# First unit of a chunked-attention and MLP kernel: the order of the first up matmuls, the engine of two query copies, the place of the roots and the steps of the next tiles' attention

## The chip, the cores and the metric

The kernel runs on one core of a Trainium2 chip. The metric is the device time of one execution in microseconds. A profile also has a span, from the first to the last instruction on the core; the time of an execution of the kernel before is 1.7 to 1.9 us longer than its span. Positions in time below are microseconds from the start of the span.

TensorE multiplies matrices, ScalarE and VectorE work on what it leaves in PSUM and on SBUF, GpSimd issues most loads and computes small things, and SyncE issues the stores. In the profile they are PE (PEld for its weight loads), ACT, DVE, POOL and SP; a "q" after a name is the engine's sequencer.

## The reference

A chunked attention with memory keys feeds a block of normalization, two matmuls and a residual:

```python
# attention, per chunk of 32 queries: 8 memory keys, 16 left, 32 own, 8 right
scores = scale * q_c @ k_full.T            # batch 4, heads 8, seq 768, head_dim 64
a = softmax(scores);  out_c = a @ v_full
# block on x = attention output as (4, 768, 512)
mu, var = mean(x), mean((x - mu) ** 2)
xn = (x - mu) / sqrt(var + 1e-6) * g_ln
out = x + relu(xn @ w_ch1) @ w_ch2         # 512 -> 2048 -> 512, float32 out
```

## The kernel before

The 3072 rows are 24 tiles of 128, worked off as 8 units of 3 tiles. Within a unit, steps 0 to 15 are the *up* steps: step hc makes hidden block hc, 128 of the 2048 hidden features for the unit's 384 rows, from four matmuls. Steps 16 to 27 are the *down* steps. Between them TensorE does the attention of the following unit's tiles: scores, values, a normalization on VectorE (`norm`), a transpose (`turn_x`), as its plan says. In the first unit, hidden blocks 0 to 7 are made before the steps begin, for one row tile at a time, as the tiles' attention ends. The *root* of a tile gives 1/sqrt(var), which is only wanted when the tile's output is added up.

```python
    def root(t, xi):
        i = t % 3
        nc.scalar.activation(out=junk, in_=xs[xi], func=ACTF.Square,
                             bias=nmean[i], accum_out=squares[i])
        nc.gpsimd.tensor_scalar(out=veps[i], in0=squares[i], ...)
        nc.gpsimd.tensor_tensor(out=rstd[xi], in0=veps[i], in1=mhalf, op=ALU.pow)

    def up(u, n, hc, t0=0, on_act=False):      # rows 128*t0 .. 128*n of the unit
        lo, hi = 128 * t0, 128 * n
        p = slot("mm")[:, 0 : hi - lo]         # four PSUM banks in turn
        for dt in range(4):
            nc.tensor.matmul(out=p, lhsT=..w1c[hc // 4].., rhs=xT[u % 2][:, dt, lo:hi], ...)
        # rectification to rT[hc]: ScalarE if hc is odd or on_act, else VectorE
    # ...
    turn_x(0, 0, 0, "mm")
    stay_busy(3)
    values(0, 2)
    norm(2, 2)
    for hc in range(3):
        up(0, 1, hc, 0, True)
    turn_x(0, 1, 1)
    for hc in range(3, 8):                     # block 4 needs w1c[1]
        up(0, 1, hc, 0, True)
    for hc in range(2):
        up(0, 2, hc, 1, True)
    turn_x(0, 2, 2)
    for hc in range(2, 8):
        up(0, 2, hc, 1)
    for hc in range(8):
        up(0, 3, hc, 2)
    # ... plan of the first unit
            at(7, clear_q, 1, 0)
            at(9, clear_q, 1, 1)
            at(10, clear_k, 1)
            for j in (0, 2):
                at(15, kq_block, 0, j, 6, NG, "mm")   # transposes of keys and queries,
                at(15, keep_rest)                     # copies out: keys VectorE, queries ScalarE
            for t in range(3):
                at(8 + t, root, t, t)
            # ... loads of the next batch
            attend(((17, 20, 20, 22), (18, 22, 22, 24), (21, 24, 24, 27)), "att")
    # attend: for each following tile the steps of scores, values, norm, turn_x;
    # its root three steps after turn_x, at the latest in step 27
```

Scores, values and transposes share two PSUM tiles, `att`, in turn: whoever comes next waits until the one before the last has been read. The up weights come in four quarters, `w1c[0]` to `w1c[3]`, each for four blocks.

The softmax here doesn't subtract the row's maximum and nothing guards it: scores larger than these inputs give would overflow.

Of the kernel before, what the change touches and what calls it, by code (L numbers as in the profile page):

```python
# [15 lines left out]
def kernel(  # L16
# [12 lines left out]
    nc = tc.nc  # L29
# [3 lines left out]
    NG = 12  # L33
# [47 lines left out]
    att = [ps.tile([128, 2, 512], FP32, name=f"att{i}") for i in range(2)]  # L81
    mm = [ps.tile([128, 512], FP32, name=f"mm{i}") for i in range(4)]
    turn = {"att": 0, "mm": 0}

    def slot(kind):
        lst = {"att": att, "mm": mm}[kind]
        turn[kind] = (turn[kind] + 1) % len(lst)
        return lst[turn[kind]]
# [4 lines left out]
    def free(ap, off, pattern, parts=None):  # L93

        p = list(ap.ap[0]) if parts is None else [ap.ap[0][0], parts]
        return bass.AP(tensor=ap.tensor, offset=ap.offset + off, ap=[p] + [list(x) for x in pattern])

    def as16(t):
        return t.bitcast(FP16)
# [75 lines left out]
    def turn_kq(pv, src, j, n):  # L175

        for r in range(8):
            for par in range(2):
                nc.tensor.matmul(  # L179
                    out=pv[64 * par : 64 * par + 64, n * r : n * r + n],  # L180
                    lhsT=src[0:n, 2 * j + par, r, :],
                    rhs=identity[0:n, 0:n],
                    is_transpose=True, start=True, stop=True,
                    tile_position=(0, 64 * par),
                )
# [14 lines left out]
    def keep_q(copy, pv, b, j, par, n, g0, g1):  # L200


        rows = slice(64 * par, 64 * par + 64)
        copy(  # L204
            out=free(QZ[b % 2][rows, g0, j, par, :], 0, [[512, g1 - g0], [8, 8], [1, 8]]),
            in_=free(pv[rows, :], 8 * g0, [[8, g1 - g0], [1, 8], [n, 8]]),
        )

    def kq_block(b, j, g0, g1, kind):

        pk, pq = slot("att"), None
        if kind == "att":
            pq = slot("att")
            pq = [pq[:, i, :] for i in range(2)]
        else:
            pq = [slot("mm")[:, :] for i in range(2)]
        for i in range(2):
            turn_kq(as16(pk[:, i, :]), k16[b % 2], j + i, 96)
        for i in range(2):
            turn_kq(as16(pq[i]), q16[b % 2], j + i, 96)  # L220

        def keep(i):
            keep_k(as16(pk[:, i, :]), b, j + i, 96, g0 + 1 if g0 else 0, g1)
            for par in range(2):
                keep_q(nc.scalar.copy, as16(pq[i]), b, j + i, par, 96, g0, g1)

        keep(0)
        kept_later.append(lambda: keep(1))
# [133 lines left out]
    def stay_busy(n, p=None):  # L362

        p = slot("mm") if p is None else p
        for _ in range(n):
            nc.tensor.matmul(out=p, lhsT=busy[:, 0:128], rhs=busy, start=True, stop=True)
# [3 lines left out]
    def up(u, n, hc, t0=0, on_act=False):  # L370

        lo, hi = 128 * t0, 128 * n
        p = slot("mm")[:, 0 : hi - lo]
        c, i = hc // 4, hc % 4
        for dt in range(4):
            w = w1c[c][:, dt, :]
            nc.tensor.matmul(  # L377
                out=p, lhsT=free(w, i, [[4, 128]]), rhs=xT[u % 2][:, dt, lo:hi],
                start=(dt == 0), stop=(dt == 3),
            )  # L380
        o = rT[hc][:, lo:hi]
        if hc % 2 or on_act:
            nc.scalar.activation(out=o, in_=p, func=ACTF.Relu)  # L383
        else:
            nc.vector.tensor_scalar(out=o, in0=p, scalar1=0.0, scalar2=None, op0=ALU.max)  # L385
# [170 lines left out]
    for hc in range(3):  # L556
        up(0, 1, hc, 0, True)
    turn_x(0, 1, 1)
    for hc in range(3, 8):
        up(0, 1, hc, 0, True)  # L560
    for hc in range(2):
        up(0, 2, hc, 1, True)
    turn_x(0, 2, 2)
    for hc in range(2, 8):
        up(0, 2, hc, 1)
    for hc in range(8):
        up(0, 3, hc, 2)

# [2 lines left out]
    for u, tiles in enumerate(units):  # L571
        n = len(tiles)
        following = units[u + 1] if u + 1 < len(units) else []
        plan = {}

        def at(step, fn, *args):
            plan.setdefault(step, []).append((fn, args))

        def attend(steps, kind="dma"):

            for i, (s0, s1, s2, s3) in enumerate(steps):
                t = following[i]
                at(s0, scores, t // 6, t % 6)
                at(s1, values, t // 6, t % 6)
                at(s2, norm, t % 6, t % 9)
                at(s3, turn_x, u + 1, i, t % 6, kind)
                at(min(s3 + 3, 27), root, t % 6, t % 9)

        def cross(steps, b, t0, t1, t2):

            for half in range(2):
                at(steps[half], cross_k, b, half, t0, t1)
                at(steps[2 + half], cross_q, half, t2 - 3, t2)

        def spread(step, b, t0, t1):
            for half in range(2):
                at(step + half, spread_q, b, half, t0, t1)

        if u == 0:
            at(7, clear_q, 1, 0)  # L600
            at(9, clear_q, 1, 1)
            at(10, clear_k, 1)
            at(23, clear_v, 1, nc.gpsimd)
            for j in (0, 2):
                at(15, kq_block, 0, j, 6, NG, "mm")
                at(15, keep_rest)
            for t in range(3):
                at(8 + t, root, t, t)
            for h in (0, 4):
                for which in range(2):  # L610
                    at(15, load_kq, 1, which, 0, 96, h, h + 4)
            for g in range(6):
                at(23, load_v_group, 1, g)
            attend(((17, 20, 20, 22), (18, 22, 22, 24), (21, 24, 24, 27)), "att")
            at(26, mem_cols, 1)
            at(26, v_mem, 1)
        elif u == 1:
            for j in (0, 2):
                at(5 + 3 * j, kq_block, 1, j, 0, NG, "att")
                at(7 + 3 * j, keep_rest)  # L620
            for g in range(6, NG):
                at(0, load_v_group, 1, g)
            for t in range(6):
                for which in range(2):
                    at(14, load_tokens, 2, which, t)
            attend(((16, 19, 19, 22), (17, 19, 20, 23), (21, 23, 23, 26)), "att")
        elif following:
            if u in (2, 4):
                attend(((2, 7, 7, 7), (4, 7, 8, 8), (9, 13, 13, 13)))
            else:  # L630
                attend(((9, 14, 14, 14), (11, 14, 15, 15), (16, 20, 20, 20)))
            if u == 2:
                cross((0, 0, 1, 1), 2, 0, 4, 3)
                at(8, mem_cols, 2)
                at(8, k_around, 2, 0, 4)
                for h in range(H):
                    at(8, load_v_head, 2, h)
                spread(9, 2, 0, 3)
                cross((14, 14, 15, 15), 2, 4, 6, 6)
            elif u == 3:  # L640
                at(1, v_mem, 2)
                at(1, v_around, 2)
                at(4, k_around, 2, 4, 6)
                spread(5, 2, 3, 6)
                for t in range(6):
                    for which in range(2):
                        at(24, load_tokens, 3, which, t)
            elif u == 4:
                for h in range(H):
                    at(0, load_v_head, 3, h)  # L650
                cross((14, 14, 15, 15), 3, 0, 4, 3)
                at(17, mem_cols, 3)
                at(17, v_mem, 3)
                at(17, v_around, 3)
                at(22, k_around, 3, 0, 4)
                spread(23, 3, 0, 3)
                cross((20, 21, 24, 25), 3, 4, 6, 6)
            elif u == 5:
                at(2, k_around, 3, 4, 6)
                spread(3, 3, 3, 6)  # L660
        for step in range(16 + 4 * n):
            if step < 16:
                if u or step > 7:
                    up(u, n, step)
            else:
                i, part = divmod(step - 16, 4)
                if u == 0:
                    i, part = (step - 16) % 3, (step - 16) // 3
                if following or i < n - 1:
                    down(tiles[i], i, part)  # L670
                elif part == 0:
                    down_last(tiles[i], i)
            for fn, args in plan.get(step, ()):
                fn(*args)
# [30 lines left out]
```

## Time and profile before

| | before |
|---|---|
| time, median (range) of 4 runs | 219.86 us (219.46 to 220.27) |
| span of the profile | 218.0 us |
| TensorE busy | 209.7 us, 96% |
| first up matmul | 17.92 |
| key transposes of step 15 begin | 31.13 |
| second unit's up begins | 49.87 |
| last VectorE work ends | 215.24 |

TensorE's busy share says little here: it is the gaps that can be won. The prediction shows its waits, which all lie in the first unit, and what is around them. A wait is best measured by the distance between two starts, less the distance that is normal for the first of them.

### The profile page before, as it was taken

Reading aid. Unit: us, or ns where it says so; the run is one execution under the profiler, and the core shown is the slowest. Engines: PE = TensorE matmul, PEld = TensorE weight load, DVE = VectorE, ACT = ScalarE, POOL = GpSimd, SP = SyncE. Lnnn points to the kernel's source line nnn. Section 1 sums busy time; section 2 is a strip of 40 time slices with the busy share of each in tenths; the row PEclk is TensorE's granted clock in tenths of the full one; section 3 lists DMA queues with packets and bytes.
Section 4 is the critical chain, followed back from the end, with each engine's and each line's share of the span. In section 5 each row is a group of like instructions: output and inputs, shape, how many; then the busy total and the mean of one; then the engine's idle time right before and its main releaser. Section 6 shows DMA issues by size and latency. Waiting matters only on the chain.

```text
span 218.0 us, 5088 instructions
## 1 busy us (share of the span) xinstructions
PE 209.7 (96%) x2025; PEld 129.8 (60%) x2025; DVE 116.7 (54%) x273; ACT 101.0 (46%) x211; POOL 104.7 (48%) x185
## 2 busy tenths in 40 slices
PE   7997989998999999999999999999999999999994
PEld 2556866546775577545764577447754676456553
DVE  6976673375764746723466339415385437534222
ACT  4476758535884766601555077202751165403200
POOL 7992236988794215987002999507047000300000
PEclk9999999999999999999999999999999999999999
DMA  4999999999999156995603999997673200330012
GB/s 78 181 151 206 209 205 184 200 204 226 167 139 173 64 76 144 148 148 191 81 5 96 113 183 157 155 158 102 159 154 96 96 3 13 83 114 11 0 48 99
DMA packets 87714, 27.37 MB, mean 126 GB/s; under 512 B 78297, under 2 KB 84185, under 8 KB 87642
## 3 DMA queue, kind: packets, MB, share of 16 engines
q0 software_dynamic: 62128, 14.38, 76.6%
q1 hardware_dynamic: 25562, 12.66, 26.5%
q8 instruction: 16, 0.26, 0.5%
q14 instruction: 8, 0.07, 0.1%
HBM read 28.84 MB, written 6.29 MB: 161 GB/s over the span
## 4 chain that ended last, share of the span: by engine, by line
PE 83%; POOL 4%; DMA 4%; DVE 4%; ACT 2%; issue 2%; POOLq 0%; DVEq 0%
PE mm L377 37%; PE mm L394 34%; PE att L289 4%; DMA w1c<-in_moe_w_ch_dram 4%; PE att L309 3%; PE att L179 2%; POOL V L117 2%; PE mm L412 2%; DVE QZ L436 1%; ACT QZ L204 1%; PE att L352 1%; DVE xn L329 1%; DVE xs L320 1%; DVE rT L385 1%; POOL qraw L107 1%
## 5 line engine op out<-in xcount | busy, mean ns | idle before, releaser
L377 PE MATMUL mm<-xT,w1c 128*128 128x384 f16 (+1 forms) x576 | 89.1, 309 | 2.4 <-DMA w1c<-in_moe_w_ch_dram 1.2
L394 PE MATMUL mm<-w2c,rT 128*128 128x512 f16 x368 | 83.9, 379 | 0.0
L377 PEld LDWEIGHTS <-w1c 128*128 128x128 f16 x576 | 58.8, 114 | 25.1 <-issue 1.5
L383 ACT ACTIVATE rT<-mm 128x384 f16<-128x384 f32 (+1 forms) x77 | 33.6, 443 | 71.4 <-PE mm L377 49.9
L394 PEld LDWEIGHTS <-rT 128*128 128x128 f16 x368 | 34.8, 98 | 38.3
L385 DVE TENSOR_SCALAR rT<-mm 128x384 f16<-128x384 f32 (+1 forms) x67 | 35.0, 526 | 34.8 <-PE mm L377 34.5
L401 DVE SCALAR_TENSOR_TENSOR osb<-mm,rstd,xs 128x512 f32<-128x512 f32 x23 | 17.1, 749 | 42.0 <-PE mm L394 27.7
L296 ACT ACTIVATE AT<-att,band 104x512 f16<-104x512 f32 x48 | 30.2, 684 | 11.3 <-PE att L289 11.0
L338 POOL TENSOR_SCALAR veps<-squares 128x1 f32<-128x1 f32 x24 | 5.0, 207 | 46.1 <-ACT junk L335 44.6
L117 POOL DMA_DIRECT2D V<-in_v_dram x24 | 18.4, 773 | 10.9 <-DMA w1c<-in_moe_w_ch_dram 7.7
L335 ACT ACTIVATE junk<-xs,nmean 128x512 f16<-128x512 f32 x24 | 17.3, 720 | 7.1 <-DVE nmean L326 6.7
L329 DVE SCALAR_TENSOR_TENSOR xn<-xs,nmean,g_row 128x512 f16<-128x512 f32 x24 | 18.4, 766 | 0.9
L320 DVE SCALAR_TENSOR_TENSOR xs<-att,rec 128x512 f32<-128x512 f32 x24 | 16.6, 691 | 1.0 <-DVE rec L319 0.2
L289 PEld LDWEIGHTS <-KT 128*128 128x128 f16 x192 | 12.7, 98 | 5.1 <-issue 1.4
L277 POOL COPY QZ<-kraw 64x768 f16<-64x768 f16 x16 | 13.5, 846 | 3.6 <-DMA kraw<-qraw 2.9
L289 PE MATMUL att<-QZ,KT 128*128 128x128 f16 x192 | 14.8, 219 | 0.3 <-ACT QZ L204 0.3
L342 POOL TENSOR_TENSOR rstd<-veps,mhalf 128x1 f32<-128x1 f32 x24 | 13.2, 551 | 2.0
L269 POOL COPY KT<-KT 128x128 f16<-128x128 f16 (+4 forms) x16 | 4.6, 320 | 18.3 <-DMA KT<-kraw 13.7
L123 POOL DMA_DIRECT2D V<-in_v_dram x16 | 12.0, 801 | 0.2 <-issue 0.2
L242 POOL DMA_DIRECT2D qraw<-in_q_dram x12 | 11.2, 935 | 1.3 <-PE mm L377 1.3
L242 POOL DMA_DIRECT2D kraw<-in_k_dram x12 | 11.2, 933 | 0.0
L309 PEld LDWEIGHTS <-AT 104*64 104x64 f16 x384 | 7.6, 111 | 6.1 <-ACT AT L296 2.0
(76 smaller groups left out, 134.2 us busy)
## 6 DMA issues: line engine op xcount, KB each, us to landing
out_dram<-osb SPq DMA_DIRECT2D x23, 256.0 KB, 2.4
V<-in_v_dram POOLq DMA_DIRECT2D x36, 96.0 KB, 6.5
w1c<-in_moe_w_ch_dram POOLq DMA_DIRECT2D x4, 512.0 KB, 9.6
w2c<-in_moe_w_ch_dram POOLq DMA_DIRECT2D x4, 512.0 KB, 13.7
kraw<-in_k_dram POOLq DMA_DIRECT2D x12, 128.0 KB, 4.7
qraw<-in_q_dram POOLq DMA_DIRECT2D x12, 128.0 KB, 4.7
qraw<-in_q_dram POOLq DMA_DIRECT2D x3, 384.0 KB, 10.7
kraw<-in_k_dram POOLq DMA_DIRECT2D x3, 256.0 KB, 5.7
```

The costliest lines, as they stand in the source:

```text
L117: nc.gpsimd.dma_start(out=V[b % 2][r : r + hi - lo, g, :, 0:64], in_=dram(v, b * H * HS + lo * D, [[64, hi - lo], [HS, H], [1, 64]]),)
L242: nc.gpsimd.dma_start(out=free(dst, 512 * t, [[64, H], [1, 64]]), in_=dram(src, b * H * HS + 128 * t * D, [[D, 128], [HS, H], [1, 64]]),)
L289: nc.tensor.matmul(out=p[:, gg, 128 * j : 128 * j + 128], lhsT=KT[b % 2][:, (4 * g + j) * KW : (4 * g + j) * KW + 128], rhs=QZ[b % 2][:, g ...
L296: nc.scalar.activation(out=free(a, 32 * c, [[512, 2], [64, 8], [1, 32]], KR), in_=free(p, 32 * c, [[512, 2], [64, 8], [1, 32]], KR), func= ...
L320: nc.vector.scalar_tensor_tensor(out=x.rearrange("p (h d) -> p h d", h=H), in0=free(p, 0, [[128, H], [1, 64]]), scalar=1.0, in1=free(r, 0, ...
L329: nc.vector.scalar_tensor_tensor(out=xn[i], in0=x, scalar=nmean[i], in1=g_row, op0=ALU.add, op1=ALU.mult,)
L335: nc.scalar.activation(out=junk, in_=xs[xi], func=ACTF.Square, bias=nmean[i], accum_out=squares[i],)
L377: nc.tensor.matmul(out=p, lhsT=free(w, i, [[4, 128]]), rhs=xT[u % 2][:, dt, lo:hi], start=(dt == 0), stop=(dt == 3),)
L383: nc.scalar.activation(out=o, in_=p, func=ACTF.Relu)
L385: nc.vector.tensor_scalar(out=o, in0=p, scalar1=0.0, scalar2=None, op0=ALU.max)
L394: nc.tensor.matmul(out=p, lhsT=rT[hc][:, 128 * i : 128 * i + 128], rhs=w2c[hc // 4][:, hc % 4, :], start=(hc == 0), stop=(hc == 15),)
L401: nc.vector.scalar_tensor_tensor(out=o, in0=p, scalar=rstd[t % 9], in1=xs[t % 9], op0=ALU.mult, op1=ALU.add,)
```

## The change

The intent is to take waits off TensorE in the first unit: run only the blocks of the first weight quarter on single row tiles, so that the second quarter has more time to land; spread the query copies over two engines; start the next tiles' attention a step or two earlier; and move the squares of the roots to where ScalarE is thought freer.

```diff
-    def kq_block(b, j, g0, g1, kind):
+    def kq_block(b, j, g0, g1, kind, last=nc.scalar.copy):
 ...
-                keep_q(nc.scalar.copy, as16(pq[i]), b, j + i, par, 96, g0, g1)
+                keep_q(last if i else nc.scalar.copy, as16(pq[i]), b, j + i, par, 96, g0, g1)
 ...
     turn_x(0, 1, 1)
-    for hc in range(3, 8):
-        up(0, 1, hc, 0, True)
-    for hc in range(2):
+    up(0, 1, 3, 0, True)
+    stay_busy(2)
+    for hc in range(4):
         up(0, 2, hc, 1, True)
     turn_x(0, 2, 2)
-    for hc in range(2, 8):
-        up(0, 2, hc, 1)
+    for hc in range(4, 8):
+        up(0, 2, hc)
     for hc in range(8):
         up(0, 3, hc, 2)
 ...
-                at(15, kq_block, 0, j, 6, NG, "mm")
+                at(15, kq_block, 0, j, 6, NG, "mm", nc.vector.tensor_copy if j else nc.scalar.copy)
 ...
-                at(8 + t, root, t, t)
+                at(19 + t, root, t, t)
 ...
-            attend(((17, 20, 20, 22), (18, 22, 22, 24), (21, 24, 24, 27)), "att")
+            attend(((17, 19, 19, 22), (18, 21, 21, 24), (20, 23, 23, 26)), "att")
```

## The prediction

> **What bounds the kernel now.** I first read the page's busy row per slice and its chain of work that ended last.
>
> ```profile
> PE   7997989998999999999999999999999999999994
> ...
> PE 83%; POOL 4%; DMA 4%; DVE 4%; ACT 2%; issue 2%; POOLq 0%; DVEq 0%
> ```
>
> TensorE is nearly always busy and makes up 83% of the chain, so only its idle time can be won without taking work off it. The change touches the first unit alone, which ends at 49.87 us of the 218.0 us span, when the second unit's first up matmul starts. I therefore asked who TensorE waited for between 17 and 82 us (engine, line, releaser: us in all, times, longest).
>
> ```profile
> PE mm L377 <- DMA w1c<-in_moe_w_ch_dram: 1.2, 1, 1.2
> PE mm L377 <- ACT xT L357: 0.7, 1, 0.7
> PE mm L377 <- DVE rT L385: 0.5, 1, 0.5
> PE att L289 <- ACT QZ L204: 0.3, 1, 0.3
> PE att L309 <- ACT AT L296: 0.3, 1, 0.3
> PE att L352 <- DVE xn L329: 0.2, 1, 0.2
> ```
>
> These six waits, 3.2 us in all, are the whole prize. The same view from 49 us to the end shows none but the 0.7 us one at 49.87 us. The modelled end of a matmul lies after the start of the next, so each costs more than it shows; I use distances between starts below. TensorE's timeline places them; I show four, the other two begin at 42.98 and 45.51 us (start, us, line, tile, count, idle before).
>
> ```profile
> 18.84 0.39 PE L377 MATMUL mm<-xT,w1c 128*128 128x128 f16 x4
> 20.39 1.53 PE L377 MATMUL mm<-xT,w1c 128*128 128x128 f16 x24 [1.17 <-DMA w1c<-in_moe_w_ch_dram]
> ...
> 29.74 1.46 PE L377 MATMUL mm<-xT,w1c 128*128 128x384 f16 x8 [0.55 <-DVE rT L385]
> ...
> 36.37 0.44 PE L289 MATMUL att<-QZ,KT 128*128 128x128 f16 x5 [0.32 <-ACT QZ L204]
> ...
> 49.87 4.06 PE L377 MATMUL mm<-xT,w1c 128*128 128x384 f16 x24 [0.67 <-ACT xT L357]
> ```
>
> The first wait is a transfer: the second quarter of the up weights lands at 20.35 us. The third to sixth come from how ScalarE and VectorE work off the attention of the next three tiles. Their own timelines hold what the change moves:
>
> ```profile
> 25.48 0.71 ACT L335 ACTIVATE junk<-xs,nmean 128x512 f16<-128x512 f32 x1
> ...
> 32.41 3.90 ACT L204 COPY QZ<-mm 64x384 f16<-64x384 f16 x8 [0.68 <-PE mm L179]
> ```
>
> ```profile
> 27.94 1.34 DVE L436 MEMSET QZ<- 64x1536 uint32 x1 [0.26 <-issue]
> ...
> 32.12 2.61 DVE L194 COPY KT<-att 128x352 f16<-128x352 f16 x8 [0.97 <-PE att L179]
> ```
>
> ScalarE needs 3.90 us for eight query copies, VectorE is done with its key copies at 34.73 and then idle until 40.33: the second engine has room.
>
> **What the Trainium skill says.** "TensorE: Matmul & The Clock Gate", section "Wait — 56ns, not 53.3ns?", gives warm back-to-back starts as N / 2.4 GHz plus about 2.5 ns: the trace has 55.8 ns for 128 columns and 162.5 ns for 384, which agrees, so 256 columns should take 109 ns (estimate). "ScalarE: Activation LUTs", section "What ACT_TABLE_LOAD costs", gives an activation with a pointer bias as 280 ns + 0.833 ns an element, 707 ns for 512; the squares of the roots took 720 ns, and another 190 ns instruction reads each sum. "DMA: Bandwidth & Descriptors", section "Issuing engines are not separate DMA queues", says that all transfers share 16 engines; the trace has them over 90% busy from about 5 to 48 us, so issuing one earlier need not land it earlier.
>
> **The change part by part.** I follow TensorE through the unit.
>
> *Up, chunk 0 and 1.* Before, hidden blocks 0 to 7 ran for row tile 0, so block 4 needed the second weight quarter: the gap from 19.06 (four matmuls of 56 ns after 18.84) to 20.39 us is 1.33 us. After, blocks 0 to 3 run for tile 0, then two filler matmuls (2 x 0.216 = 0.43, to 19.5), then blocks 0 to 3 for tile 1. That needs the transposed tile 1, whose copy on ScalarE ends at 19.62, so it starts at 19.67. Sixteen matmuls (0.89) and four transposes (0.22) bring 20.78, when the second quarter is there. Blocks 4 to 7 with 256 columns: 16 x 109 ns = 1.74, to 22.52. Eight blocks of tile 2: 32 x 55.8 ns = 1.79, to about 24.33. Before, this point is 25.11. Gain **0.78 us**. The sixteen fewer matmuls matter little, because columns, not count, cost time. The third and fourth quarters (landed 22.89 and 26.10) are needed at 24.33 and 26.93.
>
> *Up, blocks 8 to 15.* VectorE's chain is last rectification, clear (1.34), block 8, clear (1.34), block 10, which frees the bank for block 14. All of it follows from the point just moved, and neither clear is moved. ScalarE loses three squares here, but TensorE did not wait for it. So that wait (0.55 us in the view, 0.71 by starts: 28.87 to 29.74 where 0.16 is normal) **stays** and gain remains 0.78: key transposes at 30.35 instead of 31.13 (their data landed at 27.19 and 28.98), down steps at 33.2 instead of 33.98.
>
> *Query copies.* Two of eight go to VectorE, after its key copies, which then end at 33.95. It took 0.43 us for 256 query elements and 0.52 for 352 key elements, so two of 384 end near 35.0 (estimate). ScalarE, starting at 31.63, ends its six (0.487 apart) at 34.55 instead of 36.31. TensorE comes to the last head pair of the first scores at 35.1: no wait. Starts before are 35.83 and 36.37, 0.54 apart where 0.056 is normal: gain **0.48**. Scores end at 35.38 instead of 36.64.
>
> *Down steps 18 to 27.* Before, 36.64 to 49.87 is 13.23 us. Work in it: ten down steps of four matmuls (0.865 each) 8.65, two score groups 0.90, three value groups 1.17, three transposes 0.69: 11.41. The rest, 1.82, is the three waits (starts out of step by about 0.43, 0.41, 0.83) and small change. After, scores, values and norms come one step earlier, so that only one pair stays tight: values of tile 4 start at 40.15, VectorE needs 0.56 to begin and 1.91 for its norm (39.77 to 40.33 to 42.24 before), done at 42.62, and TensorE arrives at 42.49: 0.18 lost. The last transpose starts at 45.88 and its copy is ready 1.06 later (48.81 to 49.87 before), 46.94, when TensorE finishes the last down step at 46.97. The next unit starts at about 47.0 instead of 49.87. Gain here 1.82 - 0.18 = **1.64**.
>
> *Roots.* Three squares of 0.9 us move into ScalarE's steps 19 to 21, beside six exponentials of 0.63: 35.6 + 6 x 0.63 + 3 x 0.9 = 42.1, copy of tile 3 to 42.65. The values of tile 5 reuse its PSUM bank and come at 42.9. It fits with 0.2 to spare. GpSimd then issues the next batch's query and key loads first and finishes the roots at about 43 rather than 37.9, needed at 45.
>
> Sum: 0.78 + 0.48 + 1.64 = 2.9 us. The remaining units keep TensorE fed, so they only shift. I take off 0.2 for a wait I have overlooked: 219.97 - 2.7 = **217.3 us**, -1.2%.
>
> **The rivals.**
> 1. *ScalarE becomes the bound of steps 19 to 23.* For: 6.5 us of its work in a 7 us stretch, 0.2 us margin, and norm of tile 3 may not overwrite its mean before the first root has read it (38.97 against 39.15). Against: every use has its turn. Delays of 0.5 to 1 us would leave 217.8 to 218.3 us.
> 2. *The weights take over as the wait.* The third and fourth quarters of the down weights landed at 38.88 and 42.24; I need them at 40.54 and 44.15, 1.7 and 1.9 us later. If the loads moved 2.5 us later, 0.6 to 0.8 of the gain would go: 218 us. Against: they are issued before the moved GpSimd work.
> 3. *GpSimd's later work delays the second unit or beyond.* Its clears wait for the third root, so value loads begin at 45.8 rather than 43.4 us and the later loads about 2 us later. They are used from 65 us on and landed by 58 before. I expect nothing; if it bit, the time would stay near 219.5.
> 4. *The clear's wait goes too*, or fewer matmuls save more than I think: 216.5 us.
>
> **Range and chances.** Each part rests on starts in the trace; the unsure terms are rivals 1 and 4, each some 0.8 us, and the runs scatter by 0.4. So 216.5 to 218.4 us. For 2% faster, 215.57 us, a gain of 4.4 us is needed, more than all six waits cost together (4.2 by starts: 1.33 + 0.71 + 0.48 + 0.43 + 0.41 + 0.83), of which the 0.71 stays. Losing 2% would need a new stall of 7 us. Faster 0.03, within 2% 0.96, slower 0.01.
>
> **What would show it.** TensorE's waits after: none for the up weights; a short one for the transposed tile 1 near 19.7; the rectification wait still 0.5; none or under 0.1 for query copies; none over 0.2 for exponentials; the second unit's up at 47.0. Wrong would be a wait on down weights near 40 or 44, on the copy of tile 3, or an idle TensorE after 50 us.

## The result, and the profile after

The changed kernel took 217.93 us, median of 4 runs (217.74 to 218.26), beside 219.86 us. Ratios here are the mean time of one kernel's runs over that of the other's of the same rounds, so not quite the ratio of the medians; it is 0.9914, with a 95% interval of 0.989 to 0.9937. The gain is 1.9 us where the prediction said 2.7 (it started from 219.97, the median of the runs known by then). It lies within the range given, and within 2%.

The page of the changed kernel, busy tenths of TensorE in 40 slices and the chain that ended last:

```profile
PE   7999989999999999999999999999999999999993
...
PE 94%; DVE 3%; ACT 1%; issue 1%; ACTq 0%
```

No transfer is on the chain any more, and TensorE's share of it grew from 83% to 94%. Who TensorE waited for between 17 and 82 us, the view that had six lines before, now has one:

```profile
PE mm L377 <- DVE rT L385: 0.6, 1, 0.6
```

TensorE's timeline answers line by line to the one shown in the prediction (start, us, line, tile, count, idle before):

```profile
19.19 0.39 PE L377 MATMUL mm<-xT,w1c 128*128 128x128 f16 x4
19.42 0.59 PE L366 MATMUL mm<-busy 128*128 128x512 f16 x2
20.03 1.05 PE L377 MATMUL mm<-xT,w1c 128*128 128x128 f16 x16
...
29.31 1.46 PE L377 MATMUL mm<-xT,w1c 128*128 128x384 f16 x8 [0.55 <-DVE rT L385]
...
35.28 0.61 PE L289 MATMUL att<-QZ,KT 128*128 128x128 f16 x8
...
44.33 0.39 PE L352 MATMUL att<-identity,xn 128*128 128x128 f16 x4
...
47.37 4.06 PE L377 MATMUL mm<-xT,w1c 128*128 128x384 f16 x24
```

The wait for the second weight quarter is gone, the one for block 10's rectification stays, the first scores run all eight matmuls without a break, and the second unit begins 2.50 us earlier. ScalarE and VectorE have shared the query copies: ScalarE's eight in 3.90 us became six, VectorE adds its two after the key copies.

```profile
31.98 2.92 ACT L204 COPY QZ<-mm 64x384 f16<-64x384 f16 x6 [0.68 <-PE mm L179]
...
38.45 0.72 ACT L335 ACTIVATE junk<-xs,nmean 128x512 f16<-128x512 f32 x1
```

```profile
27.51 1.34 DVE L436 MEMSET QZ<- 64x1536 uint32 x1 [0.26 <-issue]
...
34.21 1.11 DVE L204 COPY QZ<-mm 64x384 f16<-64x384 f16 x2
```

Laid out by landmarks, with the two later profiles of the same changed kernel (the experiments after_again and after_third):

| | before | after | after_again | after_third |
|---|---|---|---|---|
| TensorE's clock at full speed from | 4.59 | 6.67 | 4.14 | 4.35 |
| first up matmul | 17.92 | 18.27 | 17.92 | 17.92 |
| from there to key transposes | 13.21 | 12.43 | 12.43 | 12.43 |
| from there to second unit's up | 18.74 | 16.67 | 16.66 | 16.66 |
| from there to end of last VectorE work | 165.37 | 165.42 | 165.38 | 165.37 |
| from there to end of span | 2.81 | 3.24 | 3.68 | 3.35 |
| span | 218.05 | 216.03 | 216.06 | 215.73 |

So the first unit became 2.85 us shorter once its first up matmul ran (0.78 + 2.07), the same in all three profiles, which is the sum of the prediction before it took 0.2 off. Units two to eight kept their length within 0.05 us. What is missing lies at the two ends of the program: a later start in one of three profiles, and 0.4 to 0.9 us more after the last arithmetic in all three.

### The profile page after: what moved, and what is told of

Same layout as the page of the kernel before. It is cut to its first block, busy times and chain, and to the rows that moved or that the text cites. A ratio compares the mean times of both kernels' runs of the same rounds, so it can differ in the third digit from the quotient of the medians.

```text
span 216.0 us, 5059 instructions
## 1 busy us (share of the span) xinstructions
PE 210.2 (97%) x2011; PEld 129.8 (60%) x2011; DVE 118.6 (55%) x274; ACT 99.7 (46%) x206; POOL 104.4 (48%) x185
## 4 chain that ended last, share of the span: by engine, by line
PE 94%; DVE 3%; ACT 1%; issue 1%; ACTq 0%
PE mm L377 37%; PE mm L394 37%; PE att L289 5%; PE att L309 3%; PE mm L366 3%; PE att L179 2%; PE mm L412 2%; PE mm L179 1%; DVE QZ L436 1%; ACT AT L296 1%; PE att L352 1%; PE att L366 1%; DVE rT L385 1%; PE mm L539 0%; DVE xn L329 0%
## 5 line engine op out<-in xcount | busy, mean ns | idle before, releaser
L377 PE MATMUL mm<-xT,w1c 128*128 128x384 f16 (+2 forms) x560 | 89.0, 313 | 0.6 <-DVE rT L385 0.6
L383 ACT ACTIVATE rT<-mm 128x384 f16<-128x384 f32 (+2 forms) x74 | 33.1, 453 | 72.4 <-PE mm L377 50.2
L385 DVE TENSOR_SCALAR rT<-mm 128x384 f16<-128x384 f32 (+2 forms) x66 | 34.9, 533 | 33.6 <-PE mm L377 33.5
L342 POOL TENSOR_TENSOR rstd<-veps,mhalf 128x1 f32<-128x1 f32 x24 | 13.7, 571 | 2.0
```

The source lines that it names most:

```text
L377: nc.tensor.matmul(out=p, lhsT=free(w, i, [[4, 128]]), rhs=xT[u % 2][:, dt, lo:hi], start=(dt == 0), stop=(dt == 3),)
L383: nc.scalar.activation(out=o, in_=p, func=ACTF.Relu)
L385: nc.vector.tensor_scalar(out=o, in0=p, scalar1=0.0, scalar2=None, op0=ALU.max)
```

## The experiments

Twelve runs, ten edited kernels and the changed one twice, all with right results, each timed in rounds beside the kernel before. They came in four calls, each on one chip; times that are compared come from one call unless it is said otherwise. All are within 2% of the kernel before. Means that differ by some 0.5 us have intervals that overlap, so the parts are read from distances within the profiles, of which the three profiles of the changed kernel agree within 0.01 us in the first unit. Means of the kernel before were 219.98, 220.04, 219.94 and 219.92 us.

### The changed kernel again: after_again and after_third

No edit.

> The changed kernel once more, to see whether the 0.6 us between forecast (217.3) and result (217.93) is real. Theory A (late start shows now): in the kernel before, the wait for the second weight quarter at 20.3 us absorbs any late start of TensorE; in the changed one nothing does, so the gain is 2.85 us less whatever the first up matmul is later than 17.9 us in that run (0.35 in the profile after, where the clock opened at 6.67 us instead of 4.59). Then the second unit's up starts 29.1 us after the first up matmul again, and the mean gain is 1.9 to 2.6 us. Theory B (the end): the last stores land 0.4 us later in the changed kernel, every time: last VectorE work to the end of the span is again 3.2 us against 2.8 before. Theory C (scatter): the gain comes out at 2.7 or more.

Measured: 217.70 us median of 4, ratio 0.9897 (0.9878 to 0.9915), a gain of 2.3 us.

> The changed kernel a third time, beside the two versions below on one chip. From the two profiles so far: up starts at 17.9 to 18.3 us, the second unit's up 29.1 us later, last VectorE work to the end of the span 3.2 to 3.7 us (2.8 if the last instruction packet comes after the end, as it did in two of six profiles with 4021 rows); mean 217.6 to 218.0 us.

Measured: 217.56 us median of 5, ratio 0.9897 (0.9882 to 0.9913). The first result, 1.9 us, was at the small end; the gain is about 2.2 us. Theory C, scatter alone, wanted 2.7 or more and falls. Theory B's longer end came back both times, 3.7 and 3.4 us. Theory A's late start did not come in these two profiles.

### Undoing one part: up_old, query_old, attend_old, roots_old

**up_old** puts the up order of the first unit back.

```diff
-    up(0, 1, 3, 0, True)
-    stay_busy(2)
-    for hc in range(4):
+    for hc in range(3, 8):
+        up(0, 1, hc, 0, True)
+    for hc in range(2):
         up(0, 2, hc, 1, True)
     turn_x(0, 2, 2)
-    for hc in range(4, 8):
-        up(0, 2, hc)
+    for hc in range(2, 8):
+        up(0, 2, hc, 1)
```

> Only the up part is undone. My working gives that part 0.78 us where TensorE starts early, 0.43 where it starts as in the profile after; the wait for the second weight quarter (about 1.3 us by starts) comes back, and the second unit's up starts near 47.8 whatever the clock did. So 0.4 to 0.8 us slower than the changed kernel. If the weights were no bound (rival: fewer, wider matmuls made the gain), there would be no wait at 20.4 us and the time would still be slower.

Measured: 218.06 us, mean 0.4 us above after_again's. The transfer's wait is back in the list of TensorE's waits:

```profile
PE mm L377 <- DMA w1c<-in_moe_w_ch_dram: 1.6, 2, 1.3
```

In this run the weights landed late (the first up matmul itself waited for its quarter and came at 18.54), and from there to the key transposes it took 13.30 us instead of 12.43. So the wait was the cost, not the count of matmuls. attend_alone, below, shows this once more: it has the old order and its sixteen more matmuls, but in its profile no wait for these weights, and the same distance was 12.08 us.

**query_old** gives the query copies back to ScalarE.

```diff
-                at(15, kq_block, 0, j, 6, NG, "mm", nc.vector.tensor_copy if j else nc.scalar.copy)
+                at(15, kq_block, 0, j, 6, NG, "mm")
```

> Only the query copies go back to ScalarE. My working: the wait of the first scores for QZ comes back at 0.5 us by starts and all that follows moves by it: 0.5 us slower than the changed kernel. Rival: with scores, values and roots packed closer, ScalarE becomes the bound and the loss is over 1 us; or the values wait for exponentials anyway and the loss is under 0.2.

Measured: 218.20 us median, mean 0.5 us above after_again's. Its first up matmul came at 17.92 as there, and its second unit's up at 47.50 instead of 47.01: 0.49 us, the term of the prediction, with the old wait in its old size:

```profile
35.59 0.44 PE L289 MATMUL att<-QZ,KT 128*128 128x128 f16 x5 [0.33 <-ACT QZ L204]
```

**attend_old** puts the steps of the attention back, and leaves the roots in the down steps.

```diff
-            attend(((17, 19, 19, 22), (18, 21, 21, 24), (20, 23, 23, 26)), "att")
+            attend(((17, 20, 20, 22), (18, 22, 22, 24), (21, 24, 24, 27)), "att")
```

> Only the steps of scores, values, norms and transposes go back, the roots stay in the down steps. My working: a wait of about 0.35 us before the transpose of tile 4 and one of about 0.85 us for the copy of tile 5 before the second unit's up, which starts about 1.0 us later than in the changed kernel: 1.0 us slower. Rival: the earlier query copies and the earlier up already removed these waits, then under 0.3 us.

Measured: 219.78 us, ratio 1.0002: nearly everything is lost, 2.3 us of mean. From the key transposes to the second unit's up it took 18.33 us instead of 16.66, so 1.67 us where I expected 1.0. The two waits that I named are there, and a third. Below are TensorE's lines in the kernel before, then in this run:

```profile
42.98 0.44 PE L309 MATMUL att<-V,AT 104*64 104x65 f16 x16 [0.27 <-ACT AT L296]
...
45.51 0.40 PE L352 MATMUL att<-identity,xn 128*128 128x128 f16 x4 [0.25 <-DVE xn L329]
```

```profile
42.05 0.44 PE L309 MATMUL att<-V,AT 104*64 104x65 f16 x16 [0.29 <-ACT AT L296]
...
44.57 0.40 PE L352 MATMUL att<-identity,xn 128*128 128x128 f16 x4 [0.25 <-DVE xn L329]
...
48.93 1.30 PE L377 MATMUL mm<-xT,w1c 128*128 128x384 f16 x7 [0.67 <-ACT xT L357]
```

With the old steps, the values of tile 4 come second after the scores of tile 5 on the two `att` tiles, so they wait for tile 5's exponentials; with the new steps they take the other `att` tile. The third wait is thus one of the six of the kernel before, with its 0.43 us by starts in the prediction, and my expectation had left it out: 0.43 + 0.41 + 0.83 is 1.67. The squares of the roots, which now stand before these exponentials, are not its cause. ScalarE's lines for the exponentials, before and then here:

```profile
41.67 1.26 ACT L296 ACTIVATE AT<-att,band 104x512 f16<-104x512 f32 x2 [2.25 <-PE att L289]
```

```profile
40.75 1.24 ACT L296 ACTIVATE AT<-att,band 104x512 f16<-104x512 f32 x2
```

They began 0.65 us after the scores of tile 5 (41.02) in the kernel before, where no square stood ahead, and 0.74 us after them (40.01) here, so the squares cost 0.09 us at most. Of the 1.97 us between the spans of the two profiles, 1.67 is this, 0.25 a later start and 0.06 a longer end.

**roots_old** puts the roots of the first three tiles back and leaves all else.

```diff
-                at(19 + t, root, t, t)
+                at(8 + t, root, t, t)
```

> The changed kernel with the roots of the first three tiles back in steps 8 to 10. My working: TensorE waits for none of them at either place, the second unit's up starts 29.1 us after the first up matmul within 0.1, the time is that of the changed kernel within 0.2 us. Rival: their squares delay ScalarE's evictions in the up steps and TensorE loses over 0.3 us there.

Measured: 217.46 us, ratio 0.9883 (0.9862 to 0.9904) beside 0.9897 for the changed kernel: the same. First up matmul to second unit's up is 29.09 us, as in the changed kernel. So moving the roots gave nothing by itself. Nothing in the other parts needed it either.

### One part alone: attend_alone

The kernel before with the new steps of the attention, nothing else.

```diff
-            attend(((17, 20, 20, 22), (18, 22, 22, 24), (21, 24, 24, 27)), "att")
+            attend(((17, 19, 19, 22), (18, 21, 21, 24), (20, 23, 23, 26)), "att")
```

> The kernel before with nothing but the new steps of scores, values, norms and transposes. My working: the waits before the transpose of tile 4 and for the copy of tile 5 and the one for the exponentials go, the others stay; the second unit's up starts near 48.0 instead of 49.87: 1.8 us faster than the kernel before, so most of the gain is this part. Rival: without the earlier query copies ScalarE is late and the new steps wait for it: under 1 us.

Measured: 218.27 us, ratio 0.992, mean 1.7 us below the kernel before. From key transposes to second unit's up it took 17.14 us instead of 18.74: 1.60. Together with the 0.49 us of query_old that is 2.09, beside 2.07 to 2.08 us of the whole change after the key transposes. The parts add up.

This run also shows what theory A says, by accident. Its clock opened at 5.21 us and fell back to half between 12.04 and 15.45, so its up began 1.2 us late:

```profile
19.12 0.86 PE L377 MATMUL mm<-xT,w1c 128*128 128x128 f16 x12
...
20.04 1.94 PE L377 MATMUL mm<-xT,w1c 128*128 128x128 f16 x28
...
31.20 0.87 PE L179 MATMUL att<-identity,kraw 96*64 96x96 f16 x32
```

It has the old up order, and its key transposes came at 31.20, only 0.07 us later than in the kernel before: there was no wait for the second weight quarter this time, the 28 matmuls of the second line, block 4's among them, run through. In the old order the wait takes up a late start. In the new order the distance to the key transposes is 12.43 us whenever the start is, so a late start costs its full length. This is shown for the old order by one profile, and for the new order by the profiles with starts at 17.92 and 18.27.

attend_alone's fall of 3.4 us made its mean clock 0.992; without such a fall no profile lies under 0.996. In the old order the executions at 0.989 to 0.992 are no slower than the others of their kernel: five of the kernel before, mean 219.92 us beside 219.98, one of up_old, 217.92 beside 218.16, and attend_alone's own, 218.39 beside 218.33. In the new order each is the slowest of its kernel or, in pad_free below, one of the two slowest: query_old 219.28 us beside 218.00, attend_old 221.29 beside 219.70, pad_rows 218.32 beside 217.52, pad_free 218.28 and 218.50 beside 217.28. So it cost 0.8 to 1.6 us there and nothing in the old order, as theory A has it; where in the execution the clock fell is on record for attend_alone alone. One of clear_nofill at 0.994 fits: 218.30 us beside 216.88.

### The wait that stayed: clear_later

The second clear of the query buffer goes from the up steps to a down step.

```diff
-            at(9, clear_q, 1, 1)
+            at(18, clear_q, 1, 1)
```

> The second clear of the query buffer moves from step 9 to step 18, where VectorE is idle for some 3 us. My working: the wait for block 8's to 10's rectification (0.71 us by starts) is gone, the second unit's up starts 0.7 us earlier after the first up matmul (28.4 us instead of 29.1), 0.6 to 0.8 us faster than the changed kernel. Rival: the clear delays the norm of tile 3 and the gain is given back: under 0.3 us.

Measured: 217.19 us, ratio 0.9866 (0.9844 to 0.9889). From the first up matmul to the second unit's up it took 28.39 us instead of 29.09: 0.70. The mean is 0.4 us below roots_old's, less than I expected, and the intervals overlap. The wait for block 10's rectification, the only one left in the changed kernel, was the two clears of 1.34 us on VectorE, as the prediction said of it.

### The end of the program: pad_rows, pad_free

SyncE's timeline has the last three stores as one entry: the start of the first issue and the time until the last issue is done. In the kernel before, then in after_again:

```profile
213.67 1.93 SPq L421 DMA_DIRECT2D out_dram<-osb  x3
```

```profile
210.82 2.81 SPq L421 DMA_DIRECT2D out_dram<-osb  x3
```

Issuing a store takes 0.33 us. In after_again one of the three took 1.56 (minimum, median and maximum in ns, then the first and last start):

```profile
L421 SPq DMA_DIRECT2D out_dram<-osb x3: 332/382/1558, 210.8 to 213.2; - x3
```

The last store, whose data was ready at 212.39, was issued at 213.24. The trace's packet records show what flew meanwhile: one instruction packet of 16,384 bytes, from 211.23 to 212.78. There are 16 such packets in an execution, on average some 245 TensorE instructions apart. The Trainium skill, "Runtime: NRT & Kernel Launch", section "Instruction fetch mechanics", says that an engine's instructions are refilled in blocks of 16 KiB, 256 instructions, so these are very likely TensorE's; it says of the cost of crossing such a boundary that it is "mostly hidden". The change made TensorE's program 28 instructions shorter (4021 rows, not 4049, as I counted them; matmuls and weight loads on the pages add up to one more each), which moves the last packet's place against the end: it began 2.04 us before TensorE's last matmul ended in the kernel before, and 0.70, 0.77 and 0.42 us before it in the three profiles of the changed kernel.

**pad_rows** brings the count back to 4049:

```diff
     up(0, 1, 3, 0, True)
-    stay_busy(2)
+    filler = slot("mm")[0:64, 0:64]
+    for _ in range(16):
+        nc.tensor.matmul(
+            out=filler, lhsT=busy[:, 0:64], rhs=busy[:, 0:64], start=True, stop=True
+        )
```

> The changed kernel, with its two fillers of 512 columns turned into sixteen of 64, so that TensorE's program has as many instructions as before the change (4049 rows, not 4021) and nothing else moves. Theory (instruction fetch): in the profiles of the changed kernel the last 16 KB instruction packet flies 0.4 to 1.2 us before TensorE's last matmul, the store issued in it takes 1.1 to 1.6 us to issue instead of 0.33, and the last store waits behind it; in the kernel before, the packet flew 2 us before the end and delayed nothing. With the rows back, the packet goes back to about 2 us before the end, last VectorE work to end of span is 2.8 to 2.9 us instead of 3.2 to 3.7, and the mean is 0.4 to 0.8 us below the changed kernel's 217.7. Rival (scatter): the end varies by itself, the mean is 217.7 within 0.2.

**pad_free** does it where TensorE waits anyway:

```diff
+                if u == 0 and step == 14:
+                    filler = slot("att")[0:64, 0, 0:64]
+                    for _ in range(14):
+                        nc.tensor.matmul(
+                            out=filler, lhsT=busy[:, 0:64], rhs=busy[:, 0:64], start=True, stop=True
+                        )
                 if u or step > 7:
                     up(u, n, step)
```

> The changed kernel with fourteen matmuls of 64 columns put before block 14 of the first unit, where TensorE waits 0.7 us for VectorE anyway: 4049 rows as in the kernel before, and no time of their own. Instruction-fetch theory: the second unit's up still 29.1 us after the first up matmul, the last instruction packet begins 1.9 to 2.0 us before TensorE's end, last VectorE work to end of span 2.8 to 2.9 us, ratio to the kernel before 0.986 to 0.9885 against 0.9897 for the changed kernel. Scatter theory: 0.9885 to 0.991.

Measured in the profiles: the packet began 1.90 and 1.91 us before TensorE's end, no issue was stretched, and the end took 2.79 and 2.81 us. In pad_free:

```profile
210.90 1.93 SPq L421 DMA_DIRECT2D out_dram<-osb  x3
```

Measured in the times: pad_rows 217.60 us (ratio 0.9891), pad_free 217.42 us (0.9902, 0.9877 to 0.9927). The profiled execution of pad_free, 216.99 us, was the fastest of its six; the others went up to 218.50. So the profiles did what the theory said, and the means did not: they are those of the changed kernel, 0.9897. Over all 14 profiles:

| kernels | packet before TensorE's end | last VectorE work to end of span |
|---|---|---|
| 4049 rows: before, up_old, attend_alone, pad_rows, pad_free | 1.90 to 2.04 us | 2.79 to 2.91 us |
| 4041 rows: clear_pad | 1.54 | 3.22 |
| 4021 rows: after, after_again, after_third, attend_old, clear_later | 0.42 to 0.77 | 3.24 to 3.74 |
| 4021 rows: query_old, roots_old; 4017: clear_nofill | after the end | 2.79 to 2.85 |

In the eight profiles with a stretched issue among the last three, it ended 0.36 to 0.37 us after the packet's end, whatever its own length (0.59 to 1.61 us). In three others, pad_rows, pad_free and attend_alone, an issue ran while the packet flew and was not stretched. That a stretched issue ends with the packet is shown by this repeated timing; what holds it back, why some issues escape, and why the packet of three kernels came only after the end, the runs don't show.

Two things lie outside the spans and explain part of the means. First, two of pad_free's six executions, 218.28 and 218.50 us, and one of pad_rows' five, 218.32, had the clock of 0.992 told of above, while none of the changed kernel's 13 was under 0.996. The other four of pad_free have a mean of 217.28 us, 0.988 of the kernel before, which is what the theory said; the other four of pad_rows have 217.52. This choice was made after the fact, so it supports the theory and doesn't show it. Second, a packet after the end is perhaps not free. In seven executions the time is 2.1 to 2.8 us longer than the span. All seven are among the 42 of kernels with 4021 or 4017 rows; there is none among the 72 of the others whose spans are on record. Two of them were profiled, roots_old and clear_nofill, and there the packet ended 2.6 and 2.4 us after the span; in query_old's profile, where it ended 1.6 us after the span, the time is 1.7 us longer as usual. So the short ends of 2.79 us flatter roots_old and clear_nofill, and a span alone can mislead; that the packet is what the execution waited for is not shown.

### The best of both: clear_pad, clear_nofill

clear_pad is clear_later with twelve of the 64-column fillers of pad_rows in place of `stay_busy(2)`; clear_nofill is clear_later without a filler.

```diff
     up(0, 1, 3, 0, True)
-    stay_busy(2)
```

> The later clear (0.71 us) with twelve fillers of 64 columns in place of two of 512, for 4041 rows. If both readings hold, the second unit's up starts 28.4 us after the first up matmul, the last instruction packet flies about 1.5 us or more before TensorE's end, last VectorE work to end of span 2.8 to 2.9 us; mean 216.5 to 217.0 us, 0.8 to 1.2 faster than the changed kernel. If the end is only scatter: 217.0 to 217.3.

> The later clear with no filler at all (4017 rows). TensorE waits for the copy of the transposed tile 1 whether it has fillers or not, so nothing changes in the up steps, the clock stays at full speed (rival: it drops and the up steps take longer). The last instruction packet moves four rows towards the end: if it then comes after the end, 2.8 us there and a mean like the padded version's, else 3.2 to 3.7 us and 217.2.

Measured on one chip with after_third (mean 217.66): clear_pad 216.64 us median, ratio 0.985 (0.983 to 0.987), and clear_nofill 217.00 us, ratio 0.9872 (0.9844 to 0.9901). Both have the 28.4 us from first up matmul to second unit's up. In clear_pad the list of TensorE's waits between 17 and 82 us is empty. The packet hit a store all the same (1.54 us before the end, end 3.22 us), so I was wrong on that half. In clear_nofill it came after the end, and the end took 2.79 us. Without fillers TensorE idles before tile 1, in place of the fillers:

```profile
20.30 1.05 PE L377 MATMUL mm<-xT,w1c 128*128 128x128 f16 x16 [0.45 <-ACT xT L357]
```

The clock stayed at full speed, so in that run the fillers protected nothing. clear_pad is faster than both kernels: 3.2 us of mean below the kernel before, 1.0 below the changed one.

## Why the prediction was right or wrong

It was right in class and range; its size, 2.7 us, was 0.8 too large by the first result and about 0.4 by the two that followed.

*Up, chunk 0 and 1: right.* 0.78 us were forecast, 13.21 less 12.43 is 0.78, and up_old has the wait back. The matmuls of 256 columns came 109 ns apart, as estimated.

*Blocks 8 to 15: right.* The wait for the rectification stayed, with 0.55 us in the view, and clear_later showed its size: 0.70.

*Query copies: right.* 0.48 us forecast, 0.49 in query_old. VectorE's two copies were 0.54 and 0.56 us long and ended in time.

*Down steps: the sum right, details wrong.* 1.64 us forecast; 2.07 less 0.49 is 1.58, and 1.60 in attend_alone. But I had put the transpose of tile 4 into step 23 and found 0.18 us lost there. The plan has it in step 24, and it did not wait. From the same slip I had the values of tile 5 reuse the bank of tile 3's transpose; by the plan they reuse that of tile 4's values.

*Roots: right that they fit, without profit.* ScalarE finished the third square at 41.95 in the profile after, 41.6 by the clock of the forecast, beside 42.1. roots_old is as fast.

*The sum: the unit right, the program not.* The second unit was to begin at 47.0 and began at 47.01 in the two profiles that started as the profile before did. The step that failed is "The remaining units keep TensorE fed, so they only shift". The units did only shift. What I treated as constant and was not is what lies outside them: the end, 0.43 to 0.87 us longer in the three profiles of the changed kernel, and the start, 0.35 us later in one of them. The 0.2 that I took off for an overlooked wait brought the number nearer by luck: there was no such wait. Of the spans, 2.85 less 0.35 less 0.43 less the 0.05 in between gives the 2.02 us between the profiles before and after.

Rival 1, ScalarE as the bound, and rival 2, the down weights, did not come true: none of their waits is in the list. Rival 3 did not either. Rival 4 named the clear's wait, which took another edit to remove.

*What stays open.* In the profiles, the longer end accounts for most of what is missing. The padded kernels had the short end in their profiles, and without the executions of lowered clock pad_free's mean is the forecast's 217.3 us, but that choice was made afterwards. How the 0.4 to 0.8 us by which the gain fell short divide between start, end and scatter is therefore not settled.

## What to carry to other kernels

Add up the waits of the bounding engine by distances between starts, part by part; here the forecasts of the up order, the query copies and the down steps each held to a tenth of a microsecond, and the one that left out a wait (attend_old) did not. A wait for a transfer early in a program can also take up the delay that came before it, as here, so its removal lays that delay bare. When a change that shortens the middle gives less than its sum, look at the very start and at the issue of the last stores, where the profile's busy rows show nothing, and compare each execution's clock, and its time less its span, before calling a difference scatter.

## What the Trainium skill lacked or had wrong

- "Runtime: NRT & Kernel Launch", section "Instruction fetch mechanics", calls the cost of a refill "mostly hidden". Here, in eight of 14 profiles, the issue of one of the last stores on SyncE took 0.59 to 1.61 us instead of 0.33 and ended 0.36 to 0.37 us after the 16 KiB packet; the end of the program was up to 0.9 us longer. I found this on no page.
- "TensorE: Matmul & The Clock Gate", section "What's actually happening", says that the window after which the clock opens is free-running, 3.4 us long, and puts the point's variation at 500 ns either way. In the 14 profiles the clock opened between 4.03 and 7.23 us, 3.2 us apart, as a whole window would give, for a program whose first matmul is always at 1.25 us. In attend_alone it fell back to half for 3.4 us. Where no transfer was waited for before it and the clock did not fall, the first up matmul came at 17.92 or 17.93 with openings up to 6.00 us, and at 18.27, 18.52 and 18.54 with openings at 6.67, 7.18 and 7.23. A late start has other causes too: in up_old, clear_later, clear_pad and attend_old TensorE had waited 0.3 to 0.6 us for a transfer.
